# Moving query masks, normalizing multiplies and part of the +95 shifts from VectorE to GpSimd in a gated mix of two attention branches

## The chip, the cores and the metric

The kernel runs on one core of a Trainium2 chip. A core has five engines with a queue each, which run in order and meet only at semaphores: TensorE (PE in the profile; its weight loads are listed as PEld), VectorE (DVE), ScalarE (ACT), GpSimd (POOL) and SyncE (SP), which issues most transfers. The metric is the device time in microseconds of one launch, the median over several runs.

## The reference

For 2048 tokens of width 512 the program computes two branches with 32 heads of 16 dimensions each, and mixes them with a gate per token:

```python
g = sigmoid((x * gate_w).sum(-1, keepdims=True))
# branch A: softmax attention
q, k, v = split(x @ A_wqkv)                      # 32 heads, 16 wide
p = softmax(q @ k.T * 16 ** -0.5)                # 2048 x 2048 per head
a = concat(p @ v) @ A_wo
# branch B: linear attention with feature maps
q, k, v = split(x @ B_wqkv)
phi = lambda t: concat([softmax(t @ w_phi), softmax(-t @ w_phi)])   # 32 features
kv, z = phi(k).T @ v, phi(k).sum(over tokens)
b = concat(phi(q) @ kv / (phi(q) @ z + 1e-6)) @ B_wo
out = g * a + (1 - g) * b
```

Inputs and output are bfloat16. Nearly all of the arithmetic is branch A: 32 x 2048 x 2048 exponentials.

## The kernel before, in words

**Units of branch A.** Queries are cut into 4 chunks of 512, heads into pairs of four-head groups, keys into 16 tiles of 128. A *pack* is one key tile for four heads and one query chunk; its four *units* are score tiles of 128 keys x 512 queries. There are 512 packs and 2048 units; 16 packs make a *group*, of which there are 32. Four heads of 16 dimensions lie side by side in the 128 partitions, two heads per 32-row strip, and a query tile is multiplied by a mask that keeps one of the two ("side"). So every query projection is written twice, once under each mask (`_proj_q`, line 669; mask multiply on VectorE, line 677). Two pairs of query tiles are held (`NQS = 4`).

**Two ways to an exponential.** Most units go to ScalarE, which takes 3 and 2 units by turns out of five PSUM banks and writes exp to SBUF (`_exp`, line 903). The units in the set `away` go to VectorE (`_vector_batch`, line 773), in batches of up to four: line 785 turns each score tile into 16-bit integers whose bits, read as bfloat16, approximate a power of two; three more instructions (line 801) each add a constant from STEPS = (31, 64, 95) to all four tiles at once; and all four versions, two of them against values scaled by RATIO (V2, line 705, made by GpSimd), are added up in the value product, so a VectorE unit has four value matmuls where a ScalarE unit has one (`_values`, line 955). `_share` (line 743) gives how many units of each group go to VectorE: FIRST for the first groups, FINAL for the last three, MIDDLE by turns between. `SPARE` says for how many of four batches the third shift (+95) is put on GpSimd; it is 0.

**Normalization.** `_norm` (line 974) turns a finished accumulator into tokens: a VectorE transpose out of PSUM (line 979), denominator times gate factor (987, 991), its reciprocal (993), the multiply (995) and a transpose back (1000). It is done for two sides at once; the last two groups of branch A, one side at a time.

**Branch B** (`_branch_b`, line 1006) handles tokens in pairs of 128-token tiles: first keys, then queries. `_b_pair` (line 1073) projects, negates (1103), takes maxima over a tree (1105, 1106), subtracts (1108), takes one exponential on ScalarE (1111), sums over a tree (1113 to 1116), takes reciprocals (1124) and multiplies (1118). Its buffers `bq` are three. `_b_fuse` (1044) multiplies the feature weights into the projection weights at the start, with eight strided copies on VectorE (1059).

**The order.** `Plan` (line 63) lists all operations with engine, cost in microseconds, dependencies and a due time in packs, and writes the five queues greedily: the operation that can start first, and among those within 0.02 us the lowest rank. It lets GpSimd's operations and the VectorE operations named in PORT (line 150) never run at the same time in its own reckoning. `_late` (134) holds TensorE work back that would delay the next score matmuls; zero matmuls (`_fill`, 962) are put in where TensorE would have gaps. `LEAD` is how many packs ahead of its use a VectorE batch is due, `K0, SK, Q0, SQ` (1004) are the start and spacing of branch B's work in packs. Semaphores carry the data dependencies alone; nothing at run time keeps GpSimd and VectorE apart.

Of the kernel before, what the change touches and what calls it, by code (L numbers as in the profile page):

```python
# [7 lines left out]
ALU = mybir.AluOpType  # L8
# [54 lines left out]
class Plan:  # L63
# [7 lines left out]
    PAD, PADS, OVER = 0.55, 3, 0.1  # L71
    SLIP, GAPS, FLOOR = -0.1, 0.7, 0.46

# [73 lines left out]

    NEAR = 0.1
    HURRY, FREE = 20, 60
    PORT = ("v_step", "b_neg", "b_max", "b_sub", "b_sum", "b_mul", "n_mul", "n_den", "kvbd")  # L150
# [221 lines left out]
class _Kernel:  # L372
# [4 lines left out]
    NQS = 4  # L377
    NA, NST, LEAD = 3, 3, 11
    KEEP = 14
    URGENT, AHEAD, SOON, REST = 4, -(1 << 30), -(1 << 30), 2  # L380
    SPARE, ALONE, EARLY = 0, 4, 6
    PVP = 7

# [28 lines left out]
    def _memory(self, ctx):  # L412
# [29 lines left out]
        self.V = sb("V", [P, 4 * NT * self.VCP + 16], BF16)  # L442
        self.V2 = sb("V2", [P, 4 * NT * self.VCP + 16], BF16)
        self.qT = sb("qT", [P, self.NQS, QCH], BF16)
        self.ET = sb("ET", [P, self.NSLOT, QCH], BF16)
# [5 lines left out]
        self.VB = sb("VB", [P, 4, 8, 65], BF16)  # L451
        self.bq = sb("bq", [P, 3, 2, 2 * D], BF16)
        self.btree = sb("btree", [P, 32, 8, 4], BF16)
# [116 lines left out]
    def _projections(self):  # L570
        op, NT, NQC = self.plan.op, self.NT, self.NQC
        B = Buf
        self.b_k0 = [B(), B()]
        self.b_kT = [[B() for _ in range(NQC)] for _ in range(4)]
        self.b_qT = [B() for _ in range(self.NQS)]
        self.b_onTA = [[B() for _ in range(4)] for _ in range(3)]
        self.b_T1 = [[B(), B()] for _ in range(2)]
        self.b_rinv, self.b_T2 = [B(), B()], [B(), B()]
        self._warm(9, None)
        op("ACT", lambda e: e.activation(self.bsum[:, 0:1], self.warm[:, 0:1], ACT.Exp), 1.5, reads=[self.b_warm],  # L580
           name="table", prio=-48)
        for j in range(NQC):
            if j == 0:
                for half, banks in enumerate(((2, 3), (4, 1))):
                    self._proj_k0(half, banks[0])
                    self._proj_q0(half, banks[1])
            else:
                self._proj_k(0, j)
            self._proj_v(0, j)
        for cp in range(1, 4):  # L590
            for j in range(NQC):
                self._proj_k(cp, j)
                self._proj_v(cp, j)
        self._gate()
# [65 lines left out]
    def _proj_k(self, cp, j):  # L660
        due = 32 * cp + 3 * j - 14.0 if cp else 4 * j - 2.0
        self._proj(lambda c: self.WA[:, 1, c, P * cp:P * cp + P],
# [6 lines left out]
    def _proj_q(self, qc, cp):  # L669
        n = qc * 4 + cp  # L670
        due = 32 * n - 14.0
        s0 = 2 * (n % (self.NQS // 2))

        lhs, rhs = lambda c: self.WA[:, 0, c, P * cp:P * cp + P], lambda c: self.xT[:, c, QCH * qc:QCH * qc + QCH]
        reads = [self.b_xT[qc], self.b_WA[0][cp > 0], self.b_mask]
        self._proj(lhs, rhs, reads,
                   [lambda e, b: e.tensor_tensor(self.qT[:, s0:s0 + 2, :], b[:, None, :].to_broadcast([P, 2, QCH]),  # L677
                                                 self.mask[:, :, None].to_broadcast([P, 2, QCH]), ALU.mult)],
                   self.c_dve(1024), due, due - 10, "qproj", [self.b_qT[s0]], urgent=32 * n - self.SOON)
        self.b_qT[s0 + 1] = self.b_qT[s0]  # L680

    def _proj_v(self, cp, j):

        op = self.plan.op
        job = Job()
        due = 32 * cp + 4 * j - (8.0 if cp else 0.5)
        mm = None
# [50 lines left out]

    FIRST = (4, 0, 10, 12, 10, 12, 12)
    MIDDLE = (12, 14)  # L740
    FINAL = (15, 16, 11)

# [231 lines left out]
    def _norm(self, br, qc, src, side, last, dst, b_dst, due, job, alone=False):  # L974
# [15 lines left out]
        else:  # L990
# [3 lines left out]
           writes=[b_rinv], name="n_rec", prio=due)  # L994
        op("DVE", lambda e: e.tensor_tensor(  # L995
            T2.rearrange("p b (s d) -> p s b d", s=2)[:, lo:hi], T1[:, lo:hi, :, 0:16],
            rinv[:, lo:hi, :, None].to_broadcast([P, n, 16, 16]), ALU.mult), 0.2 + 0.27 * n,
           reads=reads + [b_rinv], writes=[b_T2], name="n_mul", prio=due)
# [4 lines left out]

    K0, SK, Q0, SQ = 28.0, 11.75, 211.0, 15.25

    def _branch_b(self):
        op, NT, NQC = self.plan.op, self.NT, self.NQC
        B = Buf
        self.b_bq = [B() for _ in range(3)]
        self.b_WT = B()  # L1010
# [62 lines left out]
    def _b_pair(self, s, t0, due):  # L1073
        op = self.plan.op
        slot = self.n_pair % 3
        self.n_pair += 1
# [22 lines left out]
        def chain(ops, off, bufs):  # L1099
            for name, cost, fn in ops:  # L1100
                op("DVE", fn, cost, reads=bufs, writes=bufs, name=name, prio=due + off)
        spread = lambda t: t[:, :, None, :].to_broadcast([P, 32, DH, 4])
        chain([("b_neg", 0.16 + 1024 * 0.00027, lambda e: e.tensor_scalar(both[:, :, 1], both[:, :, 0], -1.0, None,
                                                                         op0=ALU.mult)),
               ("b_max", two(1024), lambda e: e.tensor_tensor(tree, x[:, :, 0:8], x[:, :, 8:16], ALU.max))]
# [171 lines left out]
```

## Time and profile before

| | us |
|---|---|
| median of 3 runs (lowest, highest) | 802.4 (802.28, 802.79) |
| the profiled execution's own time | 803.0 |
| its span, first to last instruction | 800.8 |
| TensorE busy | 773.5 |
| VectorE busy | 712.5 |
| ScalarE busy | 784.2 |
| GpSimd busy | 15.7 |

The page of the profile lists busy time of each engine with its share of the span, the chain of work that ended last (followed back from the last instruction), and groups of instructions: line, engine and operation, output and input tiles with their shapes, count, then busy time and the mean duration in ns, then the idle time just before them and what ended it. A line of the waits reads: engine and line that waited, what released it, microseconds in total, number of times, the longest. The trace also gives single instructions with start and duration, and busy times of the engines by stretch. The granted TensorE clock is 1.00 in every stretch. The nine warm-up matmuls apart, the first exponential starts at 9.3 us, and 7.9 us lie between the end of the last one and the end of the span.

### The profile page before, as it was taken

What the parts mean: (1) busy time and instruction counts of PE and PEld (TensorE: products, weight loads), DVE (VectorE), ACT (ScalarE), POOL (GpSimd) and SP (SyncE); (2) the same over time, 40 slices, a digit from 0 to 9 for tenths busy, and PEclk for the clock granted to TensorE, in tenths of its full rate; (3) what the DMA queues carried; (4) which work ended last, traced back from release to release, by engine and by line L of the source; (5) the groups of instructions that cost most, each with busy time, mean ns of one, the idle gap of its engine ahead of it and who ended that gap; (6) DMA issues with size and microseconds to landing.
All of it is one profiled execution on the core that took longest, in us unless ns stands there. A gap on an engine that the chain in (4) does not pass through costs nothing.

```text
span 800.8 us, 16804 instructions
## 1 busy us (share of the span) xinstructions
PE 773.5 (97%) x7366; PEld 236.9 (30%) x7366; DVE 712.5 (89%) x1218; ACT 784.2 (98%) x687; POOL 15.7 (2%) x28
## 2 busy tenths in 40 slices
PE   8989999999999999999999999999999999999998
PEld 3323233233322222232222323222232222222222
DVE  3549998998999999999999999999999999999994
ACT  6999999999999999999999999999999999999996
POOL 2000000000000000000000000000000000000000
PEclk9999999999999999999999999999999999999999
DMA  9600000000000000001010010100101001200000
GB/s 239 130 1 2 1 1 2 1 2 1 2 1 2 1 2 1 2 1 18 11 28 1 2 28 21 34 1 2 34 20 28 1 2 34 47 2 1 2 1 27
DMA packets 37864, 14.71 MB, mean 18 GB/s; under 512 B 32672, under 2 KB 37280, under 8 KB 37792
## 3 DMA queue, kind: packets, MB, share of 16 engines
q1 hardware_dynamic: 35920, 13.00, 7.5%
q8 instruction: 57, 0.93, 0.5%
q10 hardware_dynamic: 1872, 0.66, 0.3%
q14 instruction: 15, 0.12, 0.1%
HBM read 4.21 MB, written 2.10 MB: 8 GB/s over the span
## 4 chain that ended last, share of the span: by engine, by line
ACT 88%; PE 9%; DVE 2%; issue 0%
ACT ET L903 85%; ACT bq L1111 3%; PE ps L859 3%; PE ps L958 2%; PE ps L620 1%; DVE WB L1059 1%; PE ps L1190 1%; PE ps L1220 1%; PE ps L609 1%; PE ps L876 0%; PE ps L1054 0%; DVE vs L785 0%; PE ps L644 0%; DVE qT L677 0%; PE ps L965 0%
## 5 line engine op out<-in xcount | busy, mean ns | idle before, releaser
L903 ACT ACTIVATE ET<-ps 128x1536 bf16<-128x1536 f32 (+1 forms) x664 | 756.0, 1363 | 3.9 <-PE ps L859 3.4
L859 PE MATMUL ps<-qT,kT 32*128 32x512 bf16 x2048 | 300.0, 384 | 13.1 <-ACT ET L903 7.6
L785 DVE TENSOR_SCALAR vs<-ps 128x512 uint16<-128x512 f32 x388 | 258.4, 683 | 30.1 <-PE ps L859 26.9
L958 PE MATMUL ps<-ET,V 128*32 128x512 bf16 x1660 | 198.6, 388 | 0.0
L801 DVE TENSOR_SCALAR vs<-vs 128x2048 uint16<-128x2048 uint16 x291 | 192.5, 678 | 6.5 <-PE ps L958 6.3
L958 PE MATMUL ps<-vs,V 128*32 128x512 bf16 x1552 | 167.8, 384 | 0.4 <-DVE vs L801 0.4
L859 PEld LDWEIGHTS ps<-qT,kT 32*128 32x128 bf16 x2048 | 74.0, 91 | 264.4 <-ACT ET L903 203.2
L965 PE MATMUL ps<-kT,zero 128*32 128x512 bf16 x1144 | 108.9, 382 | 0.0
L958 PEld LDWEIGHTS ps<-ET,V 128*32 128x32 bf16 x1660 | 50.6, 94 | 97.0 <-issue 88.2
L958 PEld LDWEIGHTS ps<-vs,V 128*32 128x32 bf16 x1552 | 43.3, 95 | 56.8 <-issue 27.6
L620 PE MATMUL ps<-WB,xT 128*128 128x512 bf16 x192 | 59.3, 385 | 0.0
L979 DVE STREAM_TRANSPOSE T<-ps 128x512 f32<-128x512 f32 x64 | 44.8, 708 | 7.4 <-PE ps L958 5.3
L620 PE MATMUL ps<-xT,WA 128*128 128x512 bf16 (+1 forms) x128 | 38.4, 381 | 0.5 <-DVE WB L1059 0.5
L965 PEld LDWEIGHTS ps<-kT,zero 128*32 128x32 bf16 x1144 | 29.9, 95 | 27.1 <-issue 15.1
L1111 ACT ACTIVATE bq<-bq 128x2048 bf16<-128x2048 bf16 x16 | 32.8, 2047 | 0.0
L1086 DVE CAST bq<-ps 128x512 bf16<-128x512 f32 x32 | 21.9, 686 | 3.1 <-PE ps L620 2.3
L620 PEld LDWEIGHTS ps<-WB,xT 128*128 128x128 bf16 x192 | 14.1, 97 | 30.8 <-issue 20.8
L691 PE MATMUL ps<-WA,xT 128*128 128x128 bf16 x256 | 22.6, 221 | 0.1
L995 DVE TENSOR_TENSOR T<-T,rinv 128x512 bf16<-128x512 f32 (+1 forms) x33 | 21.9, 665 | 0.0
L677 DVE TENSOR_TENSOR qT<-ps,mask 128x1024 bf16<-128x1024 f32 x15 | 18.3, 1220 | 2.5 <-PE ps L620 2.4
L700 DVE CAST V<-ps 128x512 bf16<-128x512 f32 x16 | 11.0, 686 | 10.7 <-PE ps L691 10.7
L1190 PE MATMUL ps<-WoB,WT 128*128 128x512 bf16 x64 | 19.5, 384 | 0.1
(69 smaller groups left out, 339.2 us busy)
## 6 DMA issues: line engine op xcount, KB each, us to landing
WB<-in_B_wqkv_dram SPq DMA_DIRECT2D x1, 1536.0 KB, 8.5
out_dram<-WB SPq DMA_DIRECT2D x12, 128.0 KB, 1.7
WA<-in_A_wqkv_dram SPq DMA_DIRECT2D x3, 384.0 KB, 5.1
WoB<-in_B_wo_dram SPq DMA_DIRECT2D x8, 64.0 KB, 2.2
WoA<-in_A_wo_dram SPq DMA_DIRECT2D x1, 512.0 KB, 5.6
WA<-in_A_wqkv_dram ACTq DMA_DIRECT2D x3, 128.0 KB, 3.9
phiT<-bq SPq DMA_TRANSPOSE x16, 3.3
out_dram<-xT SPq DMA_DIRECT2D x2, 128.0 KB, 1.9
```

What stands on the lines that cost most here:

```text
L620: mm = op("PE", lambda e, c=c: e.matmul(self._bank(job)[:, 0:n], lhs(c), rhs(c), start=(c == 0), stop=(c == 3)), self.c_pe(n), reads=reads ...
L691: ins = e.matmul(self._bank(job)[:, P * tt:P * tt + P], self.xT[:, c, QCH * j + TOK * tt:QCH * j + TOK * tt + TOK], self.WA[:, 2, c, P * c ...
L785: parts.append(op("DVE", lambda e, j=j, job=job: e.tensor_scalar(va[:, j, :], self._bank(job), SCALE * LOG2E * 128.0, float(ORIGIN), op0=A ...
L801: o = op(eng, lambda e, k=k, tile=tile: e.tensor_scalar(flat(tile), flat(va), float(STEPS[k - 1]), None, op0=ALU.add), cost, reads=[b_va], ...
L859: return e.matmul(out, self.kT[32 * i:32 * i + 32, cp, kt * TOK:(kt + 1) * TOK], self.qT[32 * i:32 * i + 32, s, :], start=True, stop=True, ...
L903: o = plan.op("ACT", lambda e: e.activation(self.ET[:, a % NS:a % NS + n, :], self.ps[:, a % NR:a % NR + n, :], ACT.Exp, scale=SCALE), sel ...
L958: ins = e.matmul(self._bank(ot)[32 * i:32 * i + 32, :], v[:, v0:v0 + 32], tile, start=(kt == 0), stop=(kt == self.NT - 1), tile_position=( ...
L965: ins = e.matmul(self._bank(ot)[32 * i:32 * i + 32, :], self.zero[:], self.kT[:, 0, 0:QCH], start=False, stop=False, tile_position=(0, 32 ...
L979: t1 = op("DVE", lambda e: e.transpose(T1[:, side].rearrange("p b s -> p (b s)"), src()), 0.74, deps=last, writes=[b_T1[side]], name="n_t1 ...
L995: op("DVE", lambda e: e.tensor_tensor(T2.rearrange("p b (s d) -> p s b d", s=2)[:, lo:hi], T1[:, lo:hi, :, 0:16], rinv[:, lo:hi, :, None]. ...
L1111: op("ACT", lambda e: e.activation(flat, flat, ACT.Exp), self.c_act(2048) + 0.2, reads=[b], writes=[b], name="b_exp", prio=due + 1)
L1190: ops.append(self.plan.op("PE", lambda e, pr=pr: e.matmul(self._bank(job), self.onTB[:, pr, tt * TOK:tt * TOK + TOK], self.WoB[:, pr, :], ...
```

## The change

Three kinds of work move from VectorE to GpSimd. The query projection is copied out of PSUM once, unmasked, into a new tile `qtmp` on VectorE, and GpSimd writes the two masked tiles from it, one instruction each. The normalizing multiply of two sides goes to GpSimd. The +95 shift goes to GpSimd in the batches whose number modulo 4 is below 3. The negation in branch B stays on VectorE (`P_NEG = 0`) and gets a second operation, + 0.0. FIRST and FINAL give VectorE 18 more units, 406 in all. Buffers change: four shift tiles for three (NST), two branch B pair buffers for three. The remaining edits are due times and weights of the planner: VectorE batches are due 14 packs ahead instead of 11, query projections 24 instead of 14, key projections 20 instead of 14, and branch B starts at pack 50 instead of 28, in closer spacing.

```diff
@@ class Plan
-    SLIP, GAPS, FLOOR = -0.1, 0.7, 0.46
+    SLIP, GAPS, FLOOR = 0, 0.8, 0.46
-    NEAR = 0.1
-    HURRY, FREE = 20, 60
+    NEAR = 0.2
+    HURRY, FREE = 20, 40
@@ class _Kernel
-    NA, NST, LEAD = 3, 3, 11
-    KEEP = 14
-    URGENT, AHEAD, SOON, REST = 4, -(1 << 30), -(1 << 30), 2
-    SPARE, ALONE, EARLY = 0, 4, 6
-    PVP = 7
+    NBQ = 2
+    NA, NST, LEAD = 3, 4, 14
+    KEEP = 15
+    URGENT, AHEAD, SOON, REST = 6, -(1 << 30), -(1 << 30), 1
+    QDUE, KDUE, VDUE = 24, 20, 8
+    P_Q, P_MUL, P_NEG = 1, 1, 0
+    SPARE, ALONE, EARLY = 3, 9, 8
+    PVP = 3.5
...
+        self.qtmp = sb("qtmp", [P, 2, QCH], BF16)
...
-        self.bq = sb("bq", [P, 3, 2, 2 * D], BF16)
+        self.bq = sb("bq", [P, self.NBQ, 2, 2 * D], BF16)
...
@@ def _proj_k(self, cp, j):
-        due = 32 * cp + 3 * j - 14.0 if cp else 4 * j - 2.0
+        due = 32 * cp + 3 * j - self.KDUE if cp else 4 * j - 2.0
@@ def _proj_q(self, qc, cp):
-        due = 32 * n - 14.0
+        due = 32 * n - self.QDUE
...
+        if self.P_Q:
+            tmp, b_tmp = self.qtmp[:, n % 2, :], self.b_qtmp[n % 2]
+            o = self._proj(lhs, rhs, reads, [lambda e, b: e.tensor_copy(tmp, b)], self.c_dve(512), due, 32 * n - 30, "qproj",
+                           [b_tmp], urgent=32 * n - self.SOON)
+            o.deps += [r for r in b_tmp.readers if r not in o.deps]
+            b_tmp.readers = []
+            for side in range(2):
+                x = self.plan.op("POOL", lambda e, side=side: e.tensor_scalar(
+                    self.qT[:, s0 + side, :], tmp, self.mask[:, side:side + 1], 0.0, op0=ALU.mult, op1=ALU.add), 0.65,
+                    reads=[b_tmp, self.b_mask], writes=[self.b_qT[s0 + side]], name="qmask", prio=due + 1)
+                x.urgent = o.urgent
+            return
...
-    FIRST = (4, 0, 10, 12, 10, 12, 12)
+    FIRST = (6, 6, 12, 8, 12, 14, 14)
     MIDDLE = (12, 14)
-    FINAL = (15, 16, 11)
+    FINAL = (16, 18, 14)
@@ def _norm(self, br, qc, src, side, last, dst, b_dst, due, job, alone=False):
-        op("DVE", lambda e: e.tensor_tensor(
+        spare = self.P_MUL and n == 2
+        op("POOL" if spare else "DVE", lambda e: e.tensor_tensor(
             T2.rearrange("p b (s d) -> p s b d", s=2)[:, lo:hi], T1[:, lo:hi, :, 0:16],
-            rinv[:, lo:hi, :, None].to_broadcast([P, n, 16, 16]), ALU.mult), 0.2 + 0.27 * n,
+            rinv[:, lo:hi, :, None].to_broadcast([P, n, 16, 16]), ALU.mult), 1.3 if spare else 0.2 + 0.27 * n,
            reads=reads + [b_rinv], writes=[b_T2], name="n_mul", prio=due)
...
-    K0, SK, Q0, SQ = 28.0, 11.75, 211.0, 15.25
+    K0, SK, Q0, SQ = 50.0, 10.5, 208.0, 14.25
...
@@ def _b_pair(self, s, t0, due):
-        slot = self.n_pair % 3
+        slot = self.n_pair % self.NBQ
...
-        chain([("b_neg", 0.16 + 1024 * 0.00027, lambda e: e.tensor_scalar(both[:, :, 1], both[:, :, 0], -1.0, None,
-                                                                         op0=ALU.mult)),
+        chain([("b_neg", 0.16 + 1024 * 0.00027, lambda e: e.tensor_scalar(both[:, :, 1], both[:, :, 0], -1.0, 0.0,
+                                                                         op0=ALU.mult, op1=ALU.add)),
```

More of the change, by code (lines that the diff above doesn't have):

```diff
@@ L575, in _projections @@
         self.b_qT = [B() for _ in range(self.NQS)]
+        self.b_qtmp = [B(), B()]
         self.b_onTA = [[B() for _ in range(4)] for _ in range(3)]
@@ L678, in _proj_q @@
                                                  self.mask[:, :, None].to_broadcast([P, 2, QCH]), ALU.mult)],
-                   self.c_dve(1024), due, due - 10, "qproj", [self.b_qT[s0]], urgent=32 * n - self.SOON)
+                   self.c_dve(1024), due, 32 * n - 30, "qproj", [self.b_qT[s0]], urgent=32 * n - self.SOON)
         self.b_qT[s0 + 1] = self.b_qT[s0]
@@ L685, in _proj_v @@
         job = Job()
-        due = 32 * cp + 4 * j - (8.0 if cp else 0.5)
+        due = 32 * cp + 4 * j - (self.VDUE if cp else 0.5)
         mm = None
@@ L1008, in _branch_b @@
         B = Buf
-        self.b_bq = [B() for _ in range(3)]
+        self.b_bq = [B() for _ in range(self.NBQ)]
         self.b_WT = B()
@@ L1100, in chain @@
             for name, cost, fn in ops:
-                op("DVE", fn, cost, reads=bufs, writes=bufs, name=name, prio=due + off)
+                spare = self.P_NEG and name == "b_neg"
+                op("POOL" if spare else "DVE", fn, 1.2 if spare else cost, reads=bufs, writes=bufs, name=name,
+                   prio=due + off)
         spread = lambda t: t[:, :, None, :].to_broadcast([P, 32, DH, 4])
-        chain([("b_neg", 0.16 + 1024 * 0.00027, lambda e: e.tensor_scalar(both[:, :, 1], both[:, :, 0], -1.0, None,
-                                                                         op0=ALU.mult)),
+        chain([("b_neg", 0.16 + 1024 * 0.00027, lambda e: e.tensor_scalar(both[:, :, 1], both[:, :, 0], -1.0, 0.0,
+                                                                         op0=ALU.mult, op1=ALU.add)),
                ("b_max", two(1024), lambda e: e.tensor_tensor(tree, x[:, :, 0:8], x[:, :, 8:16], ALU.max))]
```

## The prediction

> **What bounds the kernel now.** I read, in this order, the busy shares and the chain of the page, the waits of ScalarE and of the weight loads, the groups, a table by stage, and the few places where GpSimd works today.
>
> ```profile
> PE 773.5 (97%) x7366; PEld 236.9 (30%) x7366; DVE 712.5 (89%) x1218; ACT 784.2 (98%) x687; POOL 15.7 (2%) x28
> ...
> ACT 88%; PE 9%; DVE 2%; issue 0%
> ```
>
> ScalarE is busy for 98% of the span and carries 88% of the chain that ended last. The waits say whether it is fed:
>
> ```profile
> PEld ps L859 <- ACT ET L903: 203.2, 508, 1.1
> ...
> PEld ps L958 <- DVE vs L801: 11.7, 40, 0.9
> ...
> ACT ET L903 <- PE ps L859: 3.4, 5, 1.0
> ```
>
> The score matmuls' weight loads stand 203.2 us in 508 waits behind an exponential (0.40 us each), while an exponential waits for scores five times in all. TensorE is ahead of ScalarE. The groups give the prices:
>
> ```profile
> L903 ACT ACTIVATE ET<-ps 128x1536 bf16<-128x1536 f32 (+1 forms) x664 | 756.0, 1363 | 3.9 <-PE ps L859 3.4
> L785 DVE TENSOR_SCALAR vs<-ps 128x512 uint16<-128x512 f32 x388 | 258.4, 683 | 30.1 <-PE ps L859 26.9
> L801 DVE TENSOR_SCALAR vs<-vs 128x2048 uint16<-128x2048 uint16 x291 | 192.5, 678 | 6.5 <-PE ps L958 6.3
> L958 PE MATMUL ps<-vs,V 128*32 128x512 bf16 x1552 | 167.8, 384 | 0.4 <-DVE vs L801 0.4
> L965 PE MATMUL ps<-kT,zero 128*32 128x512 bf16 x1144 | 108.9, 382 | 0.0
> L677 DVE TENSOR_TENSOR qT<-ps,mask 128x1024 bf16<-128x1024 f32 x15 | 18.3, 1220 | 2.5 <-PE ps L620 2.4
> ```
>
> Neighbours on one engine overlap slightly, so I divide busy time by count: 0.666 us for a VectorE tile's first step, 0.661 us for a shift, 0.108 us of TensorE for one value matmul. The table by stage has a row for each stretch (PE, PEld, DVE, ACT, POOL busy):
>
> ```profile
> 0.00:75.00 75.00, 67.42 (x576) 24.42 (x576) 40.62 (x62) 65.57 (x61) 8.31 (x18) 1.00 0.44 99
> 75.00:225.00 150.00, 145.05 (x1379) 48.64 (x1375) 137.68 (x234) 149.94 (x132) 7.35 (x10) 1.00 0.01 1
> 225.00:775.00 550.00, 538.96 (x5241) 156.74 (x5239) 519.77 (x898) 549.62 (x480) 0.00 (x0) 1.00 0.06 12
> 775.00:800.80 25.80, 22.11 (x179) 7.12 (x178) 14.47 (x27) 19.04 (x18) 0.00 (x0) 1.00 0.06 21
> ```
>
> In the 550 us of the middle ScalarE has 0.4 us free and VectorE 30. VectorE has room only in the first 75 us and at the end. GpSimd shows one thing of interest, the longest of its 16 scaled value copies (0.644 us at the median), beside what VectorE did:
>
> ```profile
> 115.77 1.55 POOL L705 TENSOR_SCALAR V<-V 128x544 bf16<-128x544 bf16 x1 [25.99 <-DVE V L700]
> ```
> ```profile
> 115.60 1.22 DVE L1108 TENSOR_TENSOR bq<-bq,btree 128x2048 bf16<-128x2048 bf16 x1
> ```
>
> It ends 0.50 us after VectorE's subtraction of two SBUF tensors does (115.60 + 1.22 = 116.82; 115.77 + 1.55 = 117.32), 0.9 us longer than the median. GpSimd was held up by VectorE.
>
> **The change, part by part.** *Tiles.* The middle pattern (12, 14 per group) stays. FIRST goes from 60 to 72, FINAL from 42 to 48, so 388 tiles become 406 and ScalarE's share 1660 becomes 1642: 657 exponentials for 664. In the chain 45 of them take 50.69 us, 2.253 us for a pair of five tiles, so 18 tiles are 18/5 x 2.253 = 8.1 us less on the path. This is the whole planned gain: nothing is taken from ScalarE in the middle.
>
> *VectorE.* 18 first steps more: +12.0 us. 406 tiles are 102 batches of up to four, 306 shifts; GpSimd takes the +95 of batches whose number modulo 4 is 0 to 2, which is 77, leaving 229 for 291: -62 x 0.661 = -41.0. The paired normalizing multiplies (31 of 0.681) leave: -21.0. The 15 masked query copies (1.220) become plain copies of 128x512, which cost 0.690 in the key projection: -8.0. Sum 712.5 - 58 = 654.5 us. In the middle: 56 shifts, 28 multiplies and 11 copies, 37 + 19 + 6 = 62 us less, leaving 458 of 550.
>
> *GpSimd.* 77 shifts of 2048 elements, 31 multiplies of 512, 30 masks of 512, none of them in the trace. Shift: the value copy scaled by elements is 0.644 x 2048/544 = 2.4 us, the 1024-element memset (1.03) doubled 2.06; I take 2.2, between, as one has a fixed part and the other reads nothing. Multiply: 0.6 us by the copy's rate, 1.2 if the two inputs are read in turn; I take 1.2, the dearer, since its operands are float32. Mask: 0.6. The middle holds 56 x 2.2 + 28 x 1.2 + 22 x 0.6 = 170 us of GpSimd, the run 77 x 2.2 + 31 x 1.2 + 30 x 0.6 = 225 on top of 15.7. GpSimd itself is at 30% and bounds nothing.
>
> *What GpSimd's work costs VectorE* is the open price. No row shows VectorE held up by GpSimd. Let x be the part of GpSimd's time in which VectorE stands still for it. Lower end 0: VectorE keeps 92 us free in the middle. Upper end 1: it needs 458 + 170 = 628 us for 550. Between them: the kinds that read two SBUF tensors, as in the held-up copy, or are shifts and negations, make 178 of VectorE's remaining 458 us in the middle, 39%. I take x = 0.39, meeting by chance: the written order keeps these kinds apart from GpSimd's (Plan's port time), which lowers it, and a shift becomes ready on both engines at the same moment, which raises it. VectorE then needs 458 + 66 = 524 us, as much as today's 520, and ScalarE still bounds: 0 us on the path. By the Trainium skill (SBUF — State Buffer, section "SBUF: two separate sides") VectorE and GpSimd share a port pair as an exclusive lock for a whole instruction, and the loser blocks completely; the held-up copy agrees for GpSimd's side, and no run here yet shows VectorE's.
>
> *Queues.* GpSimd's queue runs in order: a mask, a multiply or a value copy (up to 194 us) can stand behind one shift, 2.2 us. Masks: queries are due 24 packs ahead of use instead of 14; a pack is 800.8/512 = 1.56 us, so 37 us cover two masks and a shift, 3.4 us. Multiply: VectorE's back transpose waits for it and everything on VectorE's queue behind it. Bounds 0 (placed after the multiply's end) to 31 x 3.4 = 105 us of VectorE. I take 0 as the order is written with a cost of 1.3 for it, and the other end lies in x. A +95 shift is up to 2.2 - 0.66 + 0.9 = 2.4 us later; value matmuls on TensorE's queue wait for it, and the scores behind them. LEAD 14 for 11 gives 3 packs, 4.7 us. SP's queue issues the same transfers; nothing is moved past it.
>
> *The rest.* TensorE gets 18 x 4 - 18 = 54 value matmuls, 5.8 us, covered by 108.9 us of zero matmuls, which the order leaves out where it has work; without them it would be at ScalarE's pace. Two instead of three query/key buffers of branch B: pairs are 21 and 28.5 packs apart (33 and 44 us) and the reader is issued 14 packs (22 us) after a pair's due time, its transpose 3.3 us: 0. The added 0.0 in the negation: 0 to 16 x 0.26 us on VectorE (0.68 for 0.42, the rate of the maximum), taken as 0. SLIP lets other matmuls run 0.1 us closer to a score matmul, inside the 0.40 us mean lead: 0. Starting branch B 22 packs later moves the eight weight copies of 1.30 us, around which ScalarE waits 2.4 us (four of its five waits); -2.4 if they find banks free there, +2.4 if the busier stretch doubles it, 0 taken, since the copies are as long wherever they are. End: three more tiles in the last group and REST 1 put 9 more value matmuls near the last exponential, 0 to 1.0 us, taken as 0.5. New short waits of ScalarE in the middle: 0.5, as today's middle shows 0.4.
>
> Sum, against the profiled execution's own 803.0 (span 800.8): 803.0 - 8.1 + 0.5 + 0.5 = 795.9. That execution is 0.6 above the median of the runs, 802.4, so I forecast 795.3.
>
> **The rivals.**
> *Slower: VectorE, held up by GpSimd, becomes the bound in the middle.* The middle fills at x = 92/170 = 0.54, and the gain is gone at (92 + 8.1)/170 = 0.59. At x = 0.65 VectorE needs 458 + 111 = 569 us: +19, so 795.3 + 19 = 814. For it: the shift's coincidence, and 3 of 4 batches use it. Against: 281 of 458 us on VectorE are work of other kinds, most of it out of PSUM, that can lie beside GpSimd's. By the lock that the skill's SBUF page states, x = 1 would be reached only if VectorE's next instruction were always one of the blocked kinds.
> *Late +95 shifts stop TensorE.* Weight loads of value matmuls wait for shifts 40 times today, 11.7 us. If one in ten of the 77 comes 1.5 us after its turn, less 0.4 us of lead, that is 8 x 1.1 = 9 us: 804; one in six gives 14 us, 809. Against: LEAD's 4.7 us.
> *More than the tiles.* The 2.4 us of early waits vanish and the end costs nothing: 795.3 - 2.4 - 1.0 = 791.9, or less if the order trims the 7.9 us that follow the last exponential.
> *Not what it says:* the counts follow from the lists, so I give this none.
>
> **How the numbers follow.** Forecast 0.57 (own range 792.5 to 799), more gain 0.08 (789 to 792.5), late shifts 0.14 (799 to 812), VectorE bound 0.21 (804 to 830). About 0.2% (1.6 us) is what a measurement of this kernel can tell from no change. The late shifts divide into 0.03 faster, 0.03 same and 0.08 slower. Faster 0.57 + 0.08 + 0.03 = 0.68, same 0.03, slower 0.08 + 0.21 = 0.29. From 790 to 812 leaves out some 0.03 below and 0.12 above.
>
> **What would show it.** Right: about 657 exponentials, ScalarE still at 98% with a few microseconds of waits, VectorE at 90% or more of the middle although it has fewer instructions, its shifts and two-input instructions longer than now wherever GpSimd works, GpSimd near 240 us plus what it is held up. Wrong: ScalarE waiting for scores dozens of times (which of L801, L785 or the multiply stands before TensorE's wait names the rival), a shift on GpSimd above 2.4 us when nothing holds it, or VectorE idle before the back transposes.

## The result and the profile after

The changed kernel takes 1103.0 us (median; 1101.0 to 1106.3) against 802.5 us before: a ratio of 1.375, with an interval of 1.371 to 1.378. I had forecast 795.3 us, between 790 and 812. The profiled execution took 1106.3 us, its span is 1104.4 us. In the runs further down, one execution of e3 (1044.0 us) and one of e8 (2122.4 us, the one whose trace was kept, so that no wait of e8 is read) were slower than the others of the same kernel and are left out of the medians.

Busy time and chain of the page of the changed kernel, its granted clock by slice, and its costliest groups:

```profile
PE 888.3 (80%) x7622; PEld 249.0 (23%) x7699; DVE 827.9 (75%) x1143; ACT 800.4 (72%) x680; POOL 492.7 (45%) x166
...
PEclk9888888898789776796898978888978889798678
...
PE 50%; POOL 25%; DVE 13%; ACT 10%; issue 2%; POOLq 0%
...
L920 ACT ACTIVATE ET<-ps 128x1536 bf16<-128x1536 f32 (+1 forms) x657 | 769.7, 1252 | 290.7 <-PE ps L876 288.0
L818 POOL TENSOR_SCALAR vs<-vs 128x2048 uint16<-128x2048 uint16 (+1 forms) x77 | 416.0, 5403 | 417.6 <-PE ps L975 411.0
L975 PE MATMUL ps<-vs,V 128*32 128x512 bf16 x1624 | 206.6, 447 | 175.5 <-POOL vs L818 140.6
L818 DVE TENSOR_SCALAR vs<-vs 128x2048 uint16<-128x2048 uint16 (+1 forms) x229 | 269.9, 1197 | 2.7 <-PE ps L975 2.6
...
L1013 POOL TENSOR_TENSOR T<-T,rinv 128x512 bf16<-128x512 f32 x31 | 38.1, 1231 | 88.6 <-DVE rinv L1010 85.0
...
L688 POOL TENSOR_SCALAR qT<-qtmp,mask 128x512 bf16<-128x512 bf16 x30 | 23.4, 789 | 20.4 <-DVE qtmp L683 20.4
```

The counts are those of the prediction: 657 exponentials, 77 shifts, 31 multiplies and 30 masks on GpSimd, 229 shifts on VectorE. One duration is not. A +95 shift on GpSimd takes 5.40 us on average (5.37 at the median), where I had put 2.2 us. No engine is full: ScalarE, 98% busy before, is at 72% and waits 288 us for scores. GpSimd is 45% busy and still has 25% of the chain. VectorE's own shifts went from 0.678 to 1.197 us on average. The granted clock, 1.00 everywhere before, averages 0.842.

Ten microseconds of the changed kernel's trace show how these hang together. The lines give start, duration, engine and instruction, from GpSimd, VectorE, TensorE and ScalarE in turn:

```profile
331.00 5.37 POOL L818 TENSOR_SCALAR vs<-vs 128x2048 uint16<-128x2048 uint16 x1 [5.23 <-PE ps L975]
```
```profile
334.38 2.53 DVE L818 TENSOR_SCALAR vs<-vs 128x2048 uint16<-128x2048 uint16 x1
```
```profile
334.39 0.40 PE L975 MATMUL ps<-ET,V 128*32 128x512 bf16 x3
336.42 0.40 PE L975 MATMUL ps<-vs,V 128*32 128x512 bf16 x4 [1.64 <-POOL vs L818]
336.75 1.79 PE L625 MATMUL ps<-WB,xT 128*128 128x512 bf16 x4
...
339.57 0.61 PE L876 MATMUL ps<-qT,kT 32*128 32x512 bf16 x3
```
```profile
340.22 6.05 ACT L920 ACTIVATE ET<-ps 128x1536 bf16<-128x1536 f32 x5 [3.20 <-PE ps L876]
```

GpSimd's shift runs from 331.00 to 336.37. VectorE starts a shift at 334.38 and ends it at 336.91, 0.54 us after GpSimd, instead of 0.69 us after its own start. No semaphore orders these two, and yet VectorE's stands behind GpSimd's: the statement ahead of the prediction that nothing at run time keeps the two engines apart is wrong. TensorE comes to the value matmul of the late tile, and its whole queue stands for 1.64 us. Other work is next in that queue, the scores start at 339.57, and ScalarE, which takes them at 340.22, has waited 3.20 us.

### The profile page after: what moved, and what is told of

The parts are those of the page before. It is cut to its first block, busy times and chain, and to the rows that moved or that the text cites. A ratio compares the mean times of both kernels' runs of the same rounds, so it can differ in the third digit from the quotient of the medians.

```text
span 1104.4 us, 17464 instructions
## 1 busy us (share of the span) xinstructions
PE 888.3 (80%) x7622; PEld 249.0 (23%) x7699; DVE 827.9 (75%) x1143; ACT 800.4 (72%) x680; POOL 492.7 (45%) x166
## 4 chain that ended last, share of the span: by engine, by line
PE 50%; POOL 25%; DVE 13%; ACT 10%; issue 2%; POOLq 0%
POOL vs L818 25%; PE ps L975 19%; PE ps L876 15%; ACT ET L920 9%; DVE vs L818 7%; PE ps L982 5%; PE ps L625 5%; DVE vs L802 3%; PE ps L1210 1%; PE ps L1240 1%; ACT bq L1131 1%; DVE WB L1077 0%; PE ps L708 0%; PE ps L1155 0%; PE ps L893 0%
## 5 line engine op out<-in xcount | busy, mean ns | idle before, releaser
L920 ACT ACTIVATE ET<-ps 128x1536 bf16<-128x1536 f32 (+1 forms) x657 | 769.7, 1252 | 290.7 <-PE ps L876 288.0
L818 POOL TENSOR_SCALAR vs<-vs 128x2048 uint16<-128x2048 uint16 (+1 forms) x77 | 416.0, 5403 | 417.6 <-PE ps L975 411.0
L802 DVE TENSOR_SCALAR vs<-ps 128x512 uint16<-128x512 f32 x406 | 273.7, 684 | 167.2 <-PE ps L876 164.5
L975 PE MATMUL ps<-vs,V 128*32 128x512 bf16 x1624 | 206.6, 447 | 175.5 <-POOL vs L818 140.6
L876 PE MATMUL ps<-qT,kT 32*128 32x512 bf16 x2048 | 318.8, 439 | 23.2 <-ACT ET L920 8.3
L818 DVE TENSOR_SCALAR vs<-vs 128x2048 uint16<-128x2048 uint16 (+1 forms) x229 | 269.9, 1197 | 2.7 <-PE ps L975 2.6
L975 PE MATMUL ps<-ET,V 128*32 128x512 bf16 x1642 | 227.9, 441 | 2.1 <-DVE V L717 1.3
L982 PE MATMUL ps<-kT,zero 128*32 128x512 bf16 x1428 | 160.7, 447 | 0.5 <-issue 0.5
L1013 POOL TENSOR_TENSOR T<-T,rinv 128x512 bf16<-128x512 f32 x31 | 38.1, 1231 | 88.6 <-DVE rinv L1010 85.0
L688 POOL TENSOR_SCALAR qT<-qtmp,mask 128x512 bf16<-128x512 bf16 x30 | 23.4, 789 | 20.4 <-DVE qtmp L683 20.4
```

Source lines behind the costliest of these rows:

```text
L688: x = self.plan.op("POOL", lambda e, side=side: e.tensor_scalar(self.qT[:, s0 + side, :], tmp, self.mask[:, side:side + 1], 0.0, op0=ALU.m ...
L802: parts.append(op("DVE", lambda e, j=j, job=job: e.tensor_scalar(va[:, j, :], self._bank(job), SCALE * LOG2E * 128.0, float(ORIGIN), op0=A ...
L818: o = op(eng, lambda e, k=k, tile=tile: e.tensor_scalar(flat(tile), flat(va), float(STEPS[k - 1]), None, op0=ALU.add), cost, reads=[b_va], ...
L876: return e.matmul(out, self.kT[32 * i:32 * i + 32, cp, kt * TOK:(kt + 1) * TOK], self.qT[32 * i:32 * i + 32, s, :], start=True, stop=True, ...
L920: o = plan.op("ACT", lambda e: e.activation(self.ET[:, a % NS:a % NS + n, :], self.ps[:, a % NR:a % NR + n, :], ACT.Exp, scale=SCALE), sel ...
L975: ins = e.matmul(self._bank(ot)[32 * i:32 * i + 32, :], v[:, v0:v0 + 32], tile, start=(kt == 0), stop=(kt == self.NT - 1), tile_position=( ...
```

## The experiments

The times stand against runs of the kernel before on the same chip (802.3 to 802.5 us).

| run | us | ratio (interval) |
|---|---|---|
| changed kernel | 1103.0 | 1.375 (1.371 to 1.378) |
| e1, shift as add, add | 1253.4 | 1.561 (1.558 to 1.564) |
| e2, no shift on GpSimd | 798.5 | 0.995 (0.993 to 0.996) |
| e3, order knows 5.4 us | 1029.5 | 1.287 (1.280 to 1.293) |
| e5, shift as times 1.0 plus 95 | 805.7 | 1.004 (1.002 to 1.005) |
| e6, kernel before with that shift | 822.3 | 1.027 (1.022 to 1.032) |
| e7, 26 of the long shifts | 918.8 | 1.144 (1.142 to 1.146) |
| e8, e5 with slack | 806.0 | 1.004 (1.003 to 1.006) |
| e9, e5 with a tiny shift | 795.9 | 0.992 (0.991 to 0.994) |
| e10, tiles and due times only | 813.2 | 1.013 (1.012 to 1.015) |
| e11, two of four shifts, slack | 801.0 | 0.9985 (0.9976 to 0.9994) |
| e12, long but not waited for | 1003.9 | 1.251 (1.248 to 1.255) |
| e13, multiplies only | 798.3 | 0.995 (0.993 to 0.997) |

### What makes the shift long

My first three theories were the number of operations in the instruction, the type of its data, and VectorE in its way. Two runs were to tell them apart. The first, m1, times instructions alone, in one execution (this diff and those below show only the calls that differ):

```diff
+one = lambda e, o, i, v: e.tensor_scalar(o, i, v, None, op0=ALU.add)
+two = lambda e, o, i, v: e.tensor_scalar(o, i, v, 0.0, op0=ALU.add, op1=ALU.add)
+# GpSimd alone: one and two, uint16 and bf16, 512, 1024 and 2048 elements
+# then GpSimd's 2048-element shift beside VectorE's shifts, PSUM copies, sums of two SBUF tensors
```

> A kernel that only times instructions; it computes none of the outputs. GpSimd alone first: add of a constant over 512, 1024 and 2048 elements, in uint16 and in bfloat16, written with one operation and with two (the second adds 0.0); then the 2048-element shift beside VectorE's shifts, beside its copies out of PSUM and beside its sums of two SBUF tensors. Theory A (the form written with one operation is the slow one): one operation 5.4 us at 2048 elements in both types, two operations near 2.2 to 2.4 us (the value copy's 0.644 us scaled from 544 elements). Theory B (the type is the slow one): 5.4 us for uint16 in both forms, near 2.3 for bfloat16. Theory C (VectorE holds it up): all forms near 2.3 us alone, and 5.4 us only in the parts beside VectorE. Beside it, VectorE's shift (0.68 us alone) should take as long as the GpSimd shift in whose way it comes, up to 6 us, and the copies out of PSUM stay at 0.69.

The groups of m1 by form (L25 is the form with one addition, L26 the one with two; bbf and abf are bfloat16). In uint16 the groups mix GpSimd alone with the parts beside VectorE, so for these the single instructions are shown, three on end with start and duration:

```profile
72.60 16.26 POOL L25 TENSOR_SCALAR b<-a 128x2048 uint16<-128x2048 uint16 x3
88.94 21.43 POOL L26 TENSOR_SCALAR b<-a 128x2048 uint16<-128x2048 uint16 x3
```
```profile
L26 POOL TENSOR_SCALAR bbf<-abf 128x2048 bf16<-128x2048 bf16 x3 | 21.3, 7087 | 0.2
L25 POOL TENSOR_SCALAR bbf<-abf 128x2048 bf16<-128x2048 bf16 x3 | 16.1, 5363 | 0.2
```

GpSimd alone needs 5.36 us for one addition and 7.09 us for two, in bfloat16; three uint16 ones on end took 16.26 and 21.43 us, which is the same with the 0.08 us between them. So it is not the type, VectorE is not needed for it, and a second addition makes it longer. All three theories are out. In the whole kernel, on GpSimd and on VectorE:

```diff
-e.tensor_scalar(flat(tile), flat(va), float(STEPS[k - 1]), None, op0=ALU.add)
+e.tensor_scalar(flat(tile), flat(va), float(STEPS[k - 1]), 0.0, op0=ALU.add, op1=ALU.add)
```

> The changed kernel with one edit: the shifts have a second operation that adds 0.0, on GpSimd and on VectorE; order and waits are the same. Theory A (form): GpSimd's shift falls from 5.37 us to about 2.3, near the 2.19 that the order was written with, the 140.6 us that TensorE waits for it go, the granted clock returns to 1.00, and the time is 795 us (790 to 812). Theory B (type) and theory C (held up by VectorE): 1103 us, nothing changes. If VectorE's shifts lose their speed with two operations (0.68 to 1.2 us), its load rises by 229 x 0.5 = 115 us and the time would be near 870 even under A.

Measured 1253.4 us, with GpSimd's shift at a median of 7.08 us: neither of the two expectations. It is the same list of instructions in the same order, and the time follows GpSimd's shift. VectorE's shifts, which have the second addition too, are not longer for it (median 0.686 us, 0.685 in e2).

What the short instructions on GpSimd have in common is a multiplication: value copy and mask are "times, plus". m2 asked that question:

```diff
+fma    = lambda e, o, i, v: e.tensor_scalar(o, i, 1.0, v, op0=ALU.mult, op1=ALU.add)
+mul    = lambda e, o, i, v: e.tensor_scalar(o, i, 1.0, None, op0=ALU.mult)
+mulmul = lambda e, o, i, v: e.tensor_scalar(o, i, 1.0, 1.0, op0=ALU.mult, op1=ALU.mult)
+addmul = lambda e, o, i, v: e.tensor_scalar(o, i, v, 1.0, op0=ALU.add, op1=ALU.mult)
```

> A kernel that only times instructions; it computes none of the outputs. GpSimd alone, in uint16 at 512, 1024 and 2048 elements: x times 1.0 plus a constant; x times 1.0 alone; x times 1.0 times 1.0; a constant added and then times 1.0; and the first of these in bfloat16. Then 8 shifts in the form times 1.0 plus 95 beside VectorE's shifts, its copies out of PSUM and its sums of two SBUF tensors. The earlier kernel showed 5.36 us for one addition and 7.08 us for two at 2048 elements in both types, against 0.644 us for 544 elements in the value copy, which multiplies and then adds. Theory D (a multiplication followed by an addition has a fast way of its own): the first form 2.2 to 2.4 us in both types, the other three 5.3 to 7.1. Theory E (what is slow is the constant operand, or anything that is not bfloat16 times a number): uint16 slow in the first form too. Beside it, each VectorE shift that meets one takes about 2.3 + 0.4 us instead of 0.69.

The groups of m2 by form, 2048 elements, again one execution (L26 fma in bfloat16, L27 mul, L28 mulmul, L29 addmul):

```profile
L27 POOL TENSOR_SCALAR b<-a 128x2048 uint16<-128x2048 uint16 x3 | 16.1, 5365 | 0.2
...
L26 POOL TENSOR_SCALAR bbf<-abf 128x2048 bf16<-128x2048 bf16 x3 | 5.7, 1901 | 0.2
L29 POOL TENSOR_SCALAR b<-a 128x2048 uint16<-128x2048 uint16 x3 | 5.7, 1900 | 0.2
L28 POOL TENSOR_SCALAR b<-a 128x2048 uint16<-128x2048 uint16 x3 | 5.7, 1899 | 0.2
```

1.90 us for any of the three pairs with a multiplication, 5.37 us for a multiplication alone. Three uint16 shifts in the form "times, plus" on end took 5.87 us, as in bfloat16, so theory E is out. Theory D was right on that pair and too narrow: the other two pairs are as short. What is long is one operation alone, or two additions. In the changed kernel, for GpSimd only:

```diff
-e.tensor_scalar(flat(tile), flat(va), float(STEPS[k - 1]), None, op0=ALU.add)
+e.tensor_scalar(flat(tile), flat(va), 1.0, float(STEPS[k - 1]), op0=ALU.mult, op1=ALU.add)
```

> The changed kernel with one edit: GpSimd's +95 shift is written as times 1.0 plus 95.0, the form of its value copies; order, waits and VectorE's shifts are the same. Theory D (the pair of operations decides): GpSimd's shift near 2.3 us, TensorE's waits for it under 10 us, granted clock 1.00, and 795 us (791 to 800), a little under the 798.5 of the same kernel without the shift on GpSimd. Theory E: 1100 us. If the port shared with VectorE matters even at 2.3 us: VectorE's 229 shifts average 0.9 us or more and the time is above 805.

Measured 805.7 us, above the 791 to 800 of theory D, and VectorE's shifts average 0.739 us (busy time over count), below the 0.9 expected if the port mattered: the result lies between the two. One instruction's form is worth 1103.0 - 805.7 = 297 us here, in the same order, with the same waits. Groups of e5, and its wait of ScalarE:

```profile
L818 POOL TENSOR_SCALAR vs<-vs 128x2048 uint16<-128x2048 uint16 (+1 forms) x77 | 151.4, 1967 | 368.7 <-PE ps L977 360.7
L977 PE MATMUL ps<-ET,V 128*32 128x512 bf16 x1642 | 199.3, 388 | 0.9 <-issue 0.5
L977 PE MATMUL ps<-vs,V 128*32 128x512 bf16 x1624 | 178.7, 386 | 8.0 <-DVE vs L820 7.3
L820 DVE TENSOR_SCALAR vs<-vs 128x2048 uint16<-128x2048 uint16 (+1 forms) x229 | 169.2, 759 | 0.2
```
```profile
ACT ET L922 <- PE ps L878: 12.8, 16, 1.8
```

TensorE no longer waits for GpSimd's shift (0.4 us in all, on its weight loads), but for VectorE's shifts (L820), and ScalarE for TensorE, 12.8 us. The kernel is still slower than before, where I had forecast a gain even at 2.2 us per shift.

### What the shift on GpSimd costs at its short form

```diff
-    SPARE, ALONE, EARLY = 3, 9, 8
+    SPARE, ALONE, EARLY = 0, 9, 8
```

> The changed kernel with SPARE at 0, so all +95 shifts are on VectorE; masks, multiplies, the 406 tiles and all due times stay. If the shift on GpSimd is the whole cause: VectorE has 712.5 + 12 + 10 - 21 - 8 = 705 us of work, nothing on GpSimd is over 1.3 us, the clock is 1.00 and the time 795 to 800 us. If the masks, the multiply or the new due times and buffers take part: above 810, with TensorE or VectorE waiting for the multiply, the masks or a buffer.

798.5 us: the rest of the change is a gain of 0.5%, and three of four shifts on GpSimd take 7.2 us of it away even in the short form, although VectorE then has less to do (685.3 us busy against 709.9). The wait of ScalarE in e2:

```profile
ACT ET L920 <- PE ps L876: 3.8, 9, 1.1
```

e9 keeps the order of e5 and takes away what GpSimd holds:

```diff
-e.tensor_scalar(flat(tile), flat(va), 1.0, float(STEPS[k - 1]), op0=ALU.mult, op1=ALU.add)   # GpSimd
+e.tensor_scalar(cut(tile), cut(va), 1.0, float(STEPS[k - 1]), op0=ALU.mult, op1=ALU.add)     # GpSimd
+cut = lambda t: flat(t) if number < 4 else t[:, 0, 0:64]
```

> The kernel of 805.7 us, in the same order, with GpSimd's +95 shift cut to 64 of its 2048 elements from the fifth batch on; the rest of that tile keeps what an earlier shift left there, so this leaves out most of the +95 versions. GpSimd then holds nothing up: its 151 us of shifts become about 10. If holding VectorE up is what the shift costs: VectorE's 229 shifts return from 0.739 us to 0.67 (busy time over count), the time is 793 to 797. If the order itself costs: 803 to 806.

795.9 us. VectorE's shifts and ScalarE's wait in e9:

```profile
L821 DVE TENSOR_SCALAR vs<-vs 128x2048 uint16<-128x2048 uint16 (+1 forms) x229 | 157.6, 708 | 0.2
```
```profile
ACT ET L923 <- PE ps L879: 4.3, 7, 1.0
```

ScalarE's waits fall from 12.8 to 4.3 us, VectorE's shifts from 169.2/229 = 0.739 to 0.688 us (0.67 was expected), and 9.8 us come back. So the order and the due times are not at fault, the time that GpSimd spends in the shift is. The run does not separate a value that GpSimd delivers late from a VectorE instruction that it delays; e5 shows TensorE waiting for VectorE's (7.3 us), not GpSimd's.

e8 gave value matmuls slack behind every shift in the written order:

```diff
                 o.urgent = units[0] // 4 - self.AHEAD + 2
+                o.lat = 1.0
```

> The changed kernel with the shift on GpSimd as times 1.0 plus 95.0 (805.7 us), and the order written as if every shift, on either engine, landed 1.0 us after its end instead of 0.08 (VectorE) or 0.12 us. If the 7 us over the kernel without the shift on GpSimd (798.5) come from VectorE's shifts, held up by GpSimd, reaching the value matmuls late: ScalarE's waits for scores fall from 12.8 us to about 4, and the time is 796 to 800. If they come from the order itself or from VectorE's load: 805 as before or more.

806.0 us, no better. Whether ScalarE's waits fell is not read. The order with slack is 4.0 us longer by its own costs (791.3 for 787.3), so slack may have bought about as much as it cost; this stays open. e11 has the same slack and two of four shifts (`SPARE` 2):

> The slack of 1.0 us behind shifts, with two of four +95 shifts on GpSimd as times 1.0 plus 95.0. If slack cures the late values, this and the kernel with three of four are alike, 795 to 799, and may beat the 798.5 of none on GpSimd; if every shift on GpSimd costs in itself (7 us for 77), it lies at 801 to 803.

801.0 us, ScalarE waiting 8.2 us for scores: between none and three of four, the second of its two expectations. e6 puts the short shift alone into the kernel before:

```diff
-    SPARE, ALONE, EARLY = 0, 4, 6
+    SPARE, ALONE, EARLY = 3, 4, 6
+    # and GpSimd's shift as times 1.0 plus 95
```

> The kernel before with one part of the change alone: three of four +95 shifts on GpSimd, written as times 1.0 plus 95.0; 388 tiles, all old due times, masks and multiplies on VectorE. ScalarE has as many tiles as before, so under theory D nothing is gained: 802 to 805 us, with VectorE's busy time 40 us lower less what GpSimd holds up. If unloading VectorE were itself worth time: under 800.

822.3 us, 20 us slower, against 802 to 805 expected. VectorE is 11 us less busy (701.4), and this is the wait of ScalarE, 3.4 us before:

```profile
ACT ET L905 <- PE ps L861: 18.2, 25, 1.5
```

Unloading VectorE brings nothing here by itself, and the shift costs more than in the new order (three shift tiles and 11 packs of lead instead of four and 14; which of them matters was not tried).

### By which way the long shift costs 300 us

e3 writes the order with the true length:

```diff
-("POOL", 0.1 + n * QCH * 0.00102)
+("POOL", 0.1 + n * QCH * 0.00258)
```

> The changed kernel with one edit: the order is written with 5.38 us for GpSimd's shift of four tiles instead of 2.19. The instructions are the same, only placed otherwise. If lateness against the written order is what costs (value matmuls stand a median of 0.33 us behind the shift's planned end, and TensorE's queue stops there): TensorE's waits for the shift fall from 140.6 us to under 30, and the time falls well below 1103 but stays above 850, since VectorE's shifts and two-input work still stand aside for 77 x 5.4 = 416 us of GpSimd's. If it is the clock or the standing aside alone that costs: 1050 or more.

1029.5 us. TensorE's waits for GpSimd's shift fall from 140.6 us to 6.9, as expected of lateness, but the time only falls by 73 us. ScalarE's longest waits in e3:

```profile
ACT ET L920 <- PE ps L876: 113.7, 75, 11.7
ACT ET L920 <- PE ps L975: 82.2, 18, 11.8
```

It still waits 113.7 us for scores, 82.2 us for value matmuls that make room for its output, and 38.7 us for TensorE at the end. Most of this is in the order itself: run by its own costs, the planner ends at 941.3 us here and at 787.3 in the changed kernel, and at 793.4 with e3's costs if it is not made to keep VectorE's shifts and two-input work out of GpSimd's time. So e3 trades late shifts for a VectorE that stands aside by plan, and does not show what lateness alone costs. Knowing the length is not enough. e7 puts one of four shifts on GpSimd, in the long form (`SPARE` 1):

> The changed kernel with the slow shift (one addition, 5.4 us) on GpSimd for one batch in four: 26 shifts for 77, so 26 lateness steps. If each late shift costs TensorE's queue its own delay, as 300 us for 77 suggest (3.9 us each): 797 + 26 x 3.9 = 898 us. If the order has slack that takes up single late shifts and only their density costs: under 840.

918.8 us. Taking 798 us for none, 26 shifts cost 121 us, 4.6 us each, more than the 3.9 us that I had expected: single late shifts are not taken up either.

e12 keeps the order of the changed kernel, gives TensorE a tiny shift to wait for, and has GpSimd busy behind it with something nobody reads:

```diff
+x = Op("POOL", lambda e: e.tensor_scalar(self.side[:], self.side[:], 0.0, 0.0,
+                                         op0=ALU.add, op1=ALU.add), 5.4, "side", ...)   # behind each of the 77
```

> The changed kernel in its own order. From the fifth batch on GpSimd's +95 shift covers 64 of 2048 elements, as times 1.0 plus 95 (0.3 us), and behind each GpSimd runs a slow instruction of two additions over 1536 bytes of a tile that nobody reads (by the rates of two additions, 3.46 ns an element, about 5.3 us). It leaves out most of the +95 versions. So TensorE no longer waits for a slow shift, while GpSimd still holds VectorE up for as long. If TensorE's wait for the late shift is what costs (300 us): 810 to 850 us. If VectorE held up for 5.4 us at a time costs the same by itself, since its own late shifts stop TensorE: 950 or more, with TensorE's waits moved from GpSimd's shift to VectorE's.

1003.9 us. GpSimd's and VectorE's groups in e12, and TensorE's longest wait:

```profile
L421 POOL TENSOR_SCALAR side<-side 128x1536 uint8<-128x1536 uint8 x77 | 417.7, 5424 | 6.2
```
```profile
L836 DVE TENSOR_SCALAR vs<-vs 128x2048 uint16<-128x2048 uint16 x227 | 267.2, 1196 | 2.0 <-PE ps L993 1.9
```
```profile
PE ps L993 <- DVE vs L836: 89.5, 47, 5.0
```

Nothing waits for the long instructions themselves, and waits for the multiplies that stand behind them come to 13 us. Two thirds of the loss remain: 1003.9 - 805.7 = 198 of 297 us. VectorE's shifts are held up as much as in the changed kernel (1.196 us for four tiles at a time, 1.204 there), and now TensorE waits for those, 89.5 us for 34.0. The remaining third, 99 us, I put down to TensorE's wait for GpSimd's own shift; no run has it by itself.

A part of the loss goes with the granted TensorE clock. It is 0.842 in the changed kernel, 0.906 in e12 and 0.996 in e5, where TensorE's value matmuls wait 174.6, 89.5 and 7.3 us for shifts: in these runs it is the lower, the longer TensorE waits. The changed kernel and e5 have the same matmuls. They keep TensorE busy for 888.3 us in one and 757.3 in the other, so of the 300 us between the two spans TensorE works 131 us longer and stands idle 169 us longer. The clocks alone would let one expect 757.3 x 0.996/0.842 = 896 us of work. How much of the 131 us lies on the path was not separated.

### What the other two moves are worth

e10 is e2 with masks and multiplies back on VectorE, e13 is e2 with the masks back:

```diff
-    P_Q, P_MUL, P_NEG = 1, 1, 0
+    P_Q, P_MUL, P_NEG = 0, 0, 0    # e10
+    P_Q, P_MUL, P_NEG = 0, 1, 0    # e13
```

> The changed kernel without the three moves: shifts, masks and multiplies on VectorE; the 406 tiles, buffers and due times stay. VectorE's load rises by 21 + 8 = 29 us over the kernel without the shift on GpSimd (709.9 us busy, 798.5 us), to about 739, 93% of the span. If masks and multiplies on GpSimd make the room that the 18 tiles need: 803 to 812 us. If they are worth nothing: 797 to 800.

> The changed kernel with the shift and the query masks on VectorE, only the multiplies on GpSimd. VectorE gets 15 x 0.53 = 8 us more than with masks on GpSimd (709.9 us busy, 798.5 us). If each microsecond of VectorE counts as the step from 710 to 733 us did (14.7 us for 23): 803 us. If the multiplies alone make the room: 798 to 800.

813.2 us, 1 us above the range of its first branch, and 798.3 us, the second branch. Tiles and due times alone lose 11 us against the kernel before; the multiplies on GpSimd bring 15 us, the masks nothing. The traces show where. ScalarE's last wait, behind the last exponential, in e10 and in e2:

```profile
ACT xT L1246 <- PE ps L1240: 16.8, 2, 16.6
```
```profile
ACT xT L1246 <- PE ps L1240: 5.1, 1, 5.1
```

In e10 the last exponential ends at 791.3 us, before the 792.9 of the kernel before, and 20.4 us of the span lie behind it instead of 7.9. From 790.1 us on VectorE still has ten first steps and twelve shifts to do: it has fallen behind, and the last value matmuls and the output wait for it. Of the 15.8 us between the spans of e10 and e2, 11.4 lie there. The order that the program writes has most of this in it already: it ends at 805.5 us by its own costs in e10, at 791.8 in e13. So e13, with the 31 multiplies alone moved, is as good as any complete version here, 0.5% under the kernel before.

## Why the prediction was wrong

**The step that failed** is the price of the shift: "the value copy scaled by elements is 0.644 x 2048/544 = 2.4 us, the 1024-element memset (1.03) doubled 2.06; I take 2.2, between". It measured 5.37 us. I scaled by size across two different forms: the value copy multiplies and adds, the shift only adds. The two ends of that range lay close together, though one row multiplies and adds and the other reads nothing, and no row of the trace of before had GpSimd doing a single arithmetic operation on a tensor. The planner's own formula gives 2.19 us for the shift and 0.65 for the value copy, so it has the value copy's rate and was no second witness for my estimate. The short form measures 1.90 us. A shift on GpSimd above 2.4 us when nothing holds it was one of the signs of being wrong that the prediction named.

**The prices around it held.** The multiply takes 1.06 us at the median (I took 1.2), the mask 0.70 (0.6). The added 0.0 in the negation costs VectorE nothing (0.413 us on average in e2, 0.416 before). VectorE's load without hold-ups was put at 654.5 us; it is 670.2 in e9, which is nearly without them. ScalarE's gain was 8.1 us by the sum; its busy time fell by 6.4 us in e2 and 7.4 us in e9, with the same 657 exponentials. Of the 6.4 us in e2, 4.9 reached the span (800.8 to 795.9); ScalarE stands idle for 1.5 us more.

**GpSimd against VectorE.** I let x be the part of GpSimd's time in which VectorE stands still, took 0.39, and asked whether VectorE's load would fill the span. Comparing each of VectorE's forms that both kernels have with its mean before, the excess is about 162 us in the changed kernel, 0.33 of GpSimd's 493 us, and 26 us in e5, 0.11 of 231. The size was near for one and high for the other; the question was the wrong one. VectorE is 75% busy in the changed kernel and 85% in e5, so it never becomes the bound as the rival had it. What counts is that a held-up shift arrives late and TensorE's queue stands there, as e12 shows, where GpSimd's own shift is not late. So a second step fails at any length of the shift: the sum has 0 us on the path for what GpSimd's work costs VectorE and TensorE, and at 1.90 us, below the price that I took, the shifts on GpSimd still cost 7.2 us (e5 against e2), nearly the whole 8.1 us that the tiles were to bring. The rule that I quoted from the Trainium skill (SBUF — State Buffer, section "SBUF: two separate sides"), the loser blocks for a whole instruction, agrees for VectorE's shifts: beside GpSimd's 5.4 us they take 5.73 us in m1. For sums of two SBUF tensors m1 differs from it: they end before GpSimd's instruction does (last section).

**"Against: LEAD's 4.7 us"** was the reason to put late shifts at 0.14 and at 804 to 809 us. A due time is not slack. In the order that the program writes, the value matmul of a GpSimd shift stands, at the median, less than half a microsecond behind the shift's planned end, and the shift itself could not start early. GpSimd's waits in the changed kernel:

```profile
POOL vs L818 <- PE ps L975: 411.0, 68, 14.9
```

68 of 77 shifts waited for TensorE to free the tile they write. Four shift tiles tie the shift to TensorE's pace, whatever LEAD says. This was readable in the code and, less so, in the trace of before, where VectorE's shifts wait for TensorE only twice.

**How the length becomes time.** Four runs share one order and differ only in the shift on GpSimd (e1 also has VectorE's in its other form, which is no longer): 0.3 us gives 795.9, 1.90 gives 805.7, 5.37 gives 1103.0, 7.08 gives 1253.4. From 0.3 to 1.90 the 74 cut shifts have 118 us more on GpSimd and the time is 10 us more. From 1.90 to 5.37, 77 x 3.47 = 267 us give 297; from 5.37 to 7.08, 132 us give 150. So a microsecond of GpSimd's shifts costs 0.08 up to 1.90 us and 1.1 beyond. The order was written with 2.19; no run lies between 1.90 and 5.37, so where the price turns is not shown. My forecast of 795.3 is close to what the order does when GpSimd's shift holds next to nothing up (e9, 795.9, most of the shift left out). At 1.90 us, a little below the length that I assumed, the result is e5's 805.7, inside the range but on the other side of the kernel before.

## What to carry to other kernels

Price an instruction from a row with the same operations, not only the same engine and size, and where none exists let the range hold the engine's other rows too. In this kernel, whose order is written out beforehand, an operation longer than its planned cost lost at least its whole excess per instance (5.37 - 2.19 = 3.2 us for each shift; the kernel lost 3.9 us for each of 77 and 4.6 for each of 26), although its engine was 45% busy: the queues that wait for it are the full ones. Moving work off an engine at 89% gained nothing when the work still stood in that engine's way from outside; the move that paid, the multiplies, is one whose result no engine is seen to wait for in e2's trace, and it paid at the end of the kernel, where VectorE had fallen behind.

## What the runs showed of the hardware that I had not expected

GpSimd's time for a tensor and constants depends on the operations: per element, from the step between 1024 and 2048 elements, 0.83 ns for a pair with a multiplication ((1.900 - 1.047)/1024), 2.53 ns for one operation alone ((5.363 - 2.768)/1024), 3.38 ns for two additions ((7.087 - 3.631)/1024), the same in uint16 and bfloat16 where both were timed. On VectorE the second operation changes nothing (0.686 us for 0.685 in the shifts of e1, 0.413 for 0.416 in the negation of e2). A multiplication by 1.0 thus makes an addition 2.8 times as fast.

Beside GpSimd's one-addition shift VectorE's instructions differ by kind. These lines are from m1, a shift, copies out of PSUM and a sum of two SBUF tensors on VectorE:

```profile
149.21 5.74 DVE L25 TENSOR_SCALAR c<-a 128x2048 uint16<-128x2048 uint16 x1
```
```profile
L41 DVE CAST x<-ps 128x512 bf16<-128x512 f32 x20 | 13.8, 691 | 0.7
```
```profile
263.52 4.54 DVE L40 TENSOR_TENSOR cbf<-abf 128x2048 bf16<-128x2048 bf16 x1
```

The shift (0.69 us alone) ends 0.55 us after GpSimd's instruction (148.53 + 5.87 = 154.40). The copies are not touched (0.691 us on average, 0.684 for one alone). The sum (1.22 us alone) takes 4.54 us and ends at 268.06, 0.64 us before GpSimd's, which itself is drawn out to 6.33 us: the two overlap in part.
